# Filler matmuls, early moves and late checks around the first two attention units of a gated linear attention + multiplicative FFN kernel

## The chip, the cores and the metric

The kernel runs on one core of a Trainium2 chip, in one launch. The metric is the device time of that launch in microseconds (us), the median of 5 runs. Beside it there is one execution taken by the hardware profiler. Its engines are named as in the profile: PE (TensorE matmul), PEld (TensorE weight load), DVE (VectorE), ACT (ScalarE), POOL (GpSimd), SP (SyncE, which here issues every DMA).

## What is computed

```python
# attention: B, H, S, D = 4, 8, 768, 48
mag = sqrt(a_re**2 + a_im**2)
scale = minimum(mag, 0.999) / (mag + 1e-6)
a_re_n, a_im_n = a_re * scale, a_im * scale
for t in range(S):
    ar, ai = a_re_n[:, :, t, :, None], a_im_n[:, :, t, :, None]
    new_re, new_im = ar * S_re - ai * S_im, ar * S_im + ai * S_re
    S_re, S_im = new_re + k[:, :, t] (x) v[:, :, t], new_im
    y[:, :, t] = q[:, :, t] @ S_re
# FFN: x = y as (3072, 384); w1, w2 (384, 1024), w3 (1024, 1024), w_out (1024, 384)
out = ((x @ w1) * (x @ w2) @ w3) @ w_out
```

The four weights arrive as 64-bit floats, everything else as 32-bit floats.

## The kernel before, in words

The sequence of each of the 4 batches is cut in two, which gives 8 units (`NU`) of 384 time steps (`TT`); a unit is three chunks of 128 (`UC`). For every unit there are four kinds of work.

- **Gates** (`gates`, L531 to L643, a generator that is advanced one step at a time). ACT and DVE turn a_re and a_im into running products and angles and multiply q and k by them. Its lines that matter here: L554 (`im`, DVE, needs the loaded im), L559 (DVE), L544 (all its ACT activations), L567, L576 (scans), L600 (angle scans), L608, L616 to L620 (the last products). Its last step, "move" (L623 to L643), is 12 DMAs (L630) that rearrange k and q into KL and QL, heads beside each other, and then the loads of the next unit's k, q and v (`load_qkv`).
- **Attention** (`pieces`, L884): `turn` transposes k on PE into PSUM (tile tp, pool ps_v with 2 buffers) and ACT copies it to KT (L654); `state` multiplies KT by V (kv, L702) and DVE adds it to the running state T (L709); `scores` (sc, L664, pool ps_s with 2 buffers) needs KL and QL and is copied under the causal mask into one of two buffers A by DVE (L666); `outputs` (y, L691) needs A, T and QL, and ACT copies it to xT (L693). V is filled from the loaded vr by two ACT copies (L516).
- **FFN** (`ffn_ab`: the products with w1 and w2, tile m, L722, ACT copy a L727, DVE product ab L728, `KF` = 8 of them for a unit; `ffn_out`: tile o, L738, with w3o = w3 @ w_out, ACT copy L742 and store L744). Tiles m and o come from pool ps_m with 4 buffers.
- **Checks**: the kernel verifies that its inputs are in the range that its formulas allow. Two ACT activations per block of gates (`check_gates`, L518), and for units 0 and 1 and for all the weights a separate pass over freshly loaded data (`check_weights`, L786, tiles named look; ACT lines L520, L805, L806, L808). `judge` counts the verdicts at the end; a general slow path is behind a branch that isn't taken here.

Before the first FFN, w3o is made: 8 rows of w3 and w_out are loaded as raw 64-bit words (`row_work`, L829; tile raw, pool of 3 buffers, L758), converted by ACT (L764, L766, L770) and DVE (L768, L771, L773, L775) and multiplied on PE (`fuse`, L847, tile f). A row's w3 goes to a buffer of tag xT, of which there are two, so the conversion of row f+2 starts with a wait for PE's matmuls of row f. w1 and w2 are converted in four parts each in the same way, between the other work.

The order on PE is the order in which the Python code emits matmuls (`manual_schedule` for PE). On ACT, DVE and SP a scheduler orders the instructions ahead of time by priority and its own estimate of when they can start; on the chip each of these queues runs strictly in that fixed order, so an instruction that waits holds up all behind it. `high_priority` marks the copies out of PSUM.

The driver code is L914 to L985. After the first six rows of `fuse`, the last two rows are split: 8 matmuls for `j` 0 to 3, and four "fillers" of two matmuls each (`fill`, L941), which are put between the pieces of unit 0's attention after pieces 0, 1, 3 and 5. Then come unit 0's 8 `ffn_ab` (`rest[:HEAD]`), during which gates(1) takes its steps, and for each further unit `unit(u, ...)` (L900): `ahead` FFN parts of unit u-1 first (0 for unit 1, 3 for later ones), then the pieces of unit u with the rest of the previous unit's FFN spread evenly between them, one step of gates(u+1) after each part, and one `look` (for u > 1) after each piece.

Of the kernel before, what the change touches and what calls it, by code (L numbers as in the profile page):

```python
# [15 lines left out]
AF = mybir.ActivationFunctionType  # L16
OP = mybir.AluOpType
PSUM = bass.MemoryType.PSUM
ORDER = mybir.DependencyInfo(mybir.DependencyClass.NoSync, mybir.DependencyReason.DATA)
# [355 lines left out]
def kernel(  # L375
# [36 lines left out]
    nc = tc.nc  # L412
# [8 lines left out]
    KF = FF // P  # L421
# [21 lines left out]
    fast = ExitStack()  # L443
# [10 lines left out]
    gate_pool, head_pool = [one, None], [one, None]  # L454
# [11 lines left out]
    ONE, EPS, QUARTER, LEAST, MOST, TINY, TWO = (consts[:, i:i + 1] for i in range(7))  # L466
# [4 lines left out]
    st_low = singles.tile([P, 2, NU, KD], FP, name="st_low")  # L471
# [10 lines left out]
    def load_rows(dst, src, u, which=range(KD), queue=nc.sync):  # L482
        b, h = divmod(u, 2)
        for i, f in enumerate(which):
            queue.dma_start(out=dst[:, i, 0:TT], in_=src[b, :, DG * f:DG * (f + 1), h * TT:(h + 1) * TT].rearrange(  # L485
                "h d s -> d h s"))

    def load_gates(u):
        g = g_t.setdefault(u, {})
        for n, src in (("re", art), ("im", ait)):  # L490
            g[n] = one.tile([P, KD, TT], FP, tag=n, name=n)
            load_rows(g[n], src, u)
# [23 lines left out]
            nc.scalar.copy(out=V[:, :, :, i, e0:e0 + D], in_=vr[:, :, :, i])  # L516

    def check_gates(u, re, junk, f=0):  # L518
        for x, (scale, bias) in enumerate(((-1.0, LEAST), (1.0, MOST))):
            nc.scalar.activation(out=junk, in_=re, func=AF.Relu, scale=scale, bias=bias,  # L520
                                 accum_out=st_low[:, x, u, f:f + 1])

    chained = []

# [190 lines left out]
    def ffn_ab(u, j):  # L715
        if j == 0:
            ab_t[u] = one.tile([P, KF, TT], FP, tag="ab", name="ab")
        got = []
        for w in (w1s, w2s):
            m = ps_m.tile([P, TT], FP, tag="mm", name="m")  # L720
            for f in range(KD):
                nc.tensor.matmul(out=m, lhsT=w[:, j * P // WB, f, j * P % WB:j * P % WB + P], rhs=xT_t[u][:, f],  # L722
                                 start=(f == 0), stop=(f == KD - 1))
            got.append(m)
        a = two.tile([P, TT], FP, tag="a", name="a")
        with tc.high_priority():
            nc.scalar.copy(out=a, in_=got[0])  # L727
            nc.vector.tensor_tensor(out=ab_t[u][:, j], in0=got[1], in1=a, op=OP.mult)  # L728

    def ffn_out(u, t, parts=1):  # L730
# [46 lines left out]
    def load_weight(dst, src, halves=False):  # L777
        if src.dtype == FP:
            nc.sync.dma_start(out=dst, in_=src)
        else:  # L780
            convert(dst, src, halves)

    def words(src):
        return (src if src.dtype == FP else src.bitcast(I32)).rearrange("(i p) m -> p i m", p=P)

    def check_weights(late):  # L786

        for u in range(2):
            for f in range(KD):
                re = late.tile([P, 2, TT], FP, tag="look", name="look")  # L790
                load_rows(re, art, u, [f])
                check_gates(u, re[:, 0], re[:, 1], f)
                yield
        n = 0
        for w in (w1, w2, w3t, wo):
            if w.dtype == FP:
                continue
            src = words(w)
            step = min(src.shape[2], 1024)
            for i in range(src.shape[1]):  # L800
                for j in range(0, src.shape[2], step):
                    raw = late.tile([P, 512, 2], I32, tag="look", name="look")
                    nc.sync.dma_start(out=raw[:, 0:step // 2].rearrange("p m w -> p (m w)"), in_=src[:, i, j:j + step])
                    lo, hi = (raw[:, 0:step // 2, x].bitcast(FP) for x in range(2))
                    nc.scalar.activation(out=hi, in_=hi, func=AF.Square, scale=2.0 ** 15)  # L805
                    nc.scalar.activation(out=lo, in_=hi, func=AF.Relu, scale=-1.0, bias=TINY, accum_out=st_wts[:, n:n + 1])  # L806
                    if w is w3t:
                        nc.scalar.activation(out=hi, in_=hi, func=AF.Relu, bias=TWO, accum_out=st_wts[:, n + 40:n + 41])  # L808
                    n += 1
                    yield  # L810
# [3 lines left out]
    def rounding():  # L814

        stack = ExitStack()
        for n, k in (("raw", 3), ("low", 2)):
            cv[n] = stack.enter_context(tc.tile_pool(name=n, bufs=k))
        return stack

    def columns(src, j0, j1):
        n = 1 if src.dtype == FP else 2
        return words(src)[:, :, n * j0:n * j1]
# [5 lines left out]
    def row_work(f, parts=1):  # L829

        if f == 0:
            w3_t["wo"] = one.tile([P, KF, DM], FP, tag="ab", name="wo_s")
        w3_t[f] = two.tile([P, FF], FP, tag="xT", name="w3s")

        def some(n):
            step = FF // parts
            load_weight(w3_t[f][:, n * step:(n + 1) * step].rearrange("p (i m) -> p i m", i=1),
                        columns(w3t, n * step, (n + 1) * step)[:, f:f + 1], True)
        some(0)
        load_weight(w3_t["wo"][:, f:f + 1], words(wo)[:, f:f + 1])  # L840
        for n in range(1, parts):
            some(n)
# [34 lines left out]
        nc.vector.tensor_scalar(out=good, in0=count[:, 6:7], scalar1=float(P * need), scalar2=None, op0=OP.is_equal)  # L877

    for A in Ab:
        nc.gpsimd.memset(A, 0.0)  # L880
    for V in Vb:
        nc.gpsimd.memset(V, 0.0)

# [16 lines left out]
    def unit(u, steps, rest, look, ahead):  # L900

        for f in rest[:ahead]:
            f()
            next(steps, None)
        rest = rest[ahead:]
        p = pieces(u) + [[]]
        n = len(p)
        for i in range(n):
            for f in rest[i * len(rest) // n:(i + 1) * len(rest) // n] + p[i]:
                f()  # L910
                next(steps, None)
            next(look, None)

    gate_pool[1] = fast.enter_context(tc.tile_pool(name="late_gates", bufs=1))  # L914
    with tc.manual_schedule(engines={mybir.EngineType.PE}):

        phase = rounding()
        row_work(0, 2)
        load_gates(0)
        take_qk(0)  # L920
        steps = gates(0, True)
        for f in range(KF):
            if f:
                row_work(f)
            if f == 2:
                load_qkv(0)
            if f >= KF - 2:
                continue
            for j in range(KF):
                fuse(f, j)  # L930
            for _ in range(2):
                next(steps, None)
        work = w12_work()
        for f in work[:2]:
            f()
        for _ in steps:
            pass
        for f in range(KF - 2, KF):
            for j in range(KF // 2):
                fuse(f, j)  # L940
        fill = [lambda f=f, j=j: [fuse(f, j + x) for x in range(2)] for f in range(KF - 2, KF) for j in range(KF // 2, KF, 2)]  # L941
        load_gates(1)
        steps = gates(1, False)
        take_qk(1)
        rest = ffn(0, 2)
        work = work[2:]
        for i, p in enumerate(pieces(0)):
            for f in p:
                f()
            if i in (0, 1, 3, 5):  # L950
                fill.pop(0)()
            if i == 0:
                for f in work[:2]:
                    f()
                load_qkv(1)
            if i >= 2:
                next(steps)
            if i in (5, 7):
                work[2 + (i == 7)]()
        for i, f in enumerate(rest[:HEAD]):  # L960
            f()
            if i < 2:
                work[4 + i]()
            if i == 2:
                phase.close()
            if i < 6:
                next(steps)
        head_pool[1] = fast.enter_context(tc.tile_pool(name="late_heads", bufs=1))
        for _ in steps:
            pass  # L970
        load_gates(2)
        late = fast.enter_context(tc.tile_pool(name="late", bufs=2))
        look = check_weights(late)
        for u in range(1, NU):
            steps = gates(u + 1, False) if u + 1 < NU else iter(())
            unit(u, steps, rest[HEAD:] if u == 1 else ffn(u - 1), look if u > 1 else iter(()), AHEAD[u])
            for _ in steps:
                pass
            if u + 2 < NU:
                load_gates(u + 2)  # L980
        for _ in look:
            pass
        judge()
        for f in ffn(NU - 1):
            f()  # L985
# [41 lines left out]
```

## Time and profile before

| | |
|---|---|
| median of 5 runs | 589.92 us (588.52 to 594.95) |
| the profiled execution | 592.3 us, of which its span (first to last instruction) is 590.5 us |
| PE busy in the span | 553.0 us (94%), 3514 matmul records |
| DVE, ACT, POOL busy | 304.9, 349.6, 5.3 us |
| moved by DMA | 84.71 MB, mean 143 GB/s |
| mean granted PE clock | 0.994 |

The page of the profile cuts the span into 40 slices of 14.76 us and gives for each the busy share of every engine in tenths. A group line gives an engine's instructions of one kind, their summed busy time, the mean duration of one, and the idle time just before them with what ended it. A line of waits says which engine and line waited for which, the total, the number of times and the longest. A timeline line gives start, duration, engine, line, operation, output<-inputs, and in square brackets the idle time before it with its releaser. One program-level matmul in 32 bit shows as two records.

### The profile page before, as it was taken

Reading aid. Unit: us, or ns where it says so; the run is one execution under the profiler, and the core shown is the slowest. Engines: PE = TensorE matmul, PEld = TensorE weight load, DVE = VectorE, ACT = ScalarE, POOL = GpSimd, SP = SyncE. Lnnn points to the kernel's source line nnn. Section 1 sums busy time; section 2 is a strip of 40 time slices with the busy share of each in tenths; the row PEclk is TensorE's granted clock in tenths of the full one; section 3 lists DMA queues with packets and bytes.
Section 4 is the critical chain, followed back from the end, with each engine's and each line's share of the span. In section 5 each row is a group of like instructions: output and inputs, shape, how many; then the busy total and the mean of one; then the engine's idle time right before and its main releaser. Section 6 shows DMA issues by size and latency. Waiting matters only on the chain.

```text
span 590.5 us, 8844 instructions
## 1 busy us (share of the span) xinstructions
PE 553.0 (94%) x3514; PEld 364.9 (62%) x3514; DVE 304.9 (52%) x420; ACT 349.6 (59%) x572; POOL 5.3 (1%) x11
## 2 busy tenths in 40 slices
PE   4769989969899999999999999999999999999996
PEld 2435765548456765677567765776567656766553
DVE  6998488845761576158513674357415682310110
ACT  6897648566983699388834687498635742111100
POOL 3000000000000000000000000000000000000000
PEclk9889999999999999999999999999999999999999
DMA  8776998377385648652744348825820025000001
GB/s 296 265 295 217 247 294 279 108 183 214 122 235 117 186 136 244 127 180 87 191 114 112 117 135 188 245 78 160 199 73 1 14 68 120 1 15 29 0 1 44
DMA packets 46050, 84.71 MB, mean 143 GB/s; under 512 B 4656, under 2 KB 36144, under 8 KB 45104
## 3 DMA queue, kind: packets, MB, share of 16 engines
q1 hardware_dynamic: 46000, 84.06, 50.2%
q8 instruction: 29, 0.48, 0.3%
q14 instruction: 21, 0.17, 0.1%
HBM read 60.42 MB, written 4.72 MB: 110 GB/s over the span
## 4 chain that ended last, share of the span: by engine, by line
PE 62%; DVE 11%; DMA 10%; ACT 10%; issue 3%; SPq 3%; DVEq 0%; ACTq 0%
PE m L722 33%; PE o L738 16%; PE y L691 5%; PE sc L664 4%; DMA raw<-in_w_dram 4%; PE kv L702 3%; DMA QL<-gA 3%; ACT gZ L544 2%; PE tp L652 2%; SPq L485 2%; DVE gZ L600 2%; DMA vr<-in_v_dram 2%; ACT re L544 2%; DMA q<-in_q_dram 1%; DVE gA L576 1%
## 5 line engine op out<-in xcount | busy, mean ns | idle before, releaser
L722 PE MATMUL m<-xT,w1s 128*128 128x384 f32 x384 | 135.1, 488 | 3.9 <-ACT xT L693 3.9
L722 PE MATMUL m<-xT,w2s 128*128 128x384 f32 x384 | 134.5, 487 | 1.1 <-DVE w2s L775 0.6
L738 PE MATMUL o<-w3o,ab 128*128 128x384 f32 x384 | 130.1, 492 | 0.0
L728 DVE TENSOR_TENSOR ab<-m,a 128x384 f32<-128x384 f32 x64 | 35.5, 555 | 139.9 <-PE m L722 129.3
L722 PEld LDWEIGHTS m<-xT,w2s 128*128 128x128 f32 x384 | 72.8, 190 | 52.7 <-DVE w2s L775 1.2
L738 PEld LDWEIGHTS o<-w3o,ab 128*128 128x128 f32 x384 | 71.0, 190 | 48.5 <-issue 3.8
L722 PEld LDWEIGHTS m<-xT,w1s 128*128 128x128 f32 x384 | 70.3, 190 | 47.2 <-ACT xT L693 5.3
L727 ACT COPY a<-m 128x384 f32<-128x384 f32 x64 | 30.4, 475 | 75.7 <-PE m L722 75.6
L852 PE MATMUL f<-wo_s,w3s 128*128 128x384 f32 x128 | 48.9, 541 | 17.6 <-DVE wo_s L775 17.6
L654 ACT COPY KT<-tp 128x384 f32<-128x384 f32 x40 | 33.6, 845 | 43.5 <-PE tp L652 43.5
L664 PE MATMUL sc<-QL,KL 96*128 96x128 f32 x384 | 47.8, 278 | 2.8 <-DVE A L666 2.8
L664 PEld LDWEIGHTS sc<-QL,KL 96*128 96x128 f32 x384 | 45.6, 192 | 6.8 <-DVE A L666 4.1
L852 PEld LDWEIGHTS f<-wo_s,w3s 128*128 128x128 f32 x128 | 26.5, 213 | 37.3 <-DVE wo_s L775 19.7
L666 DVE COPY_PREDICATED A<-causal,sc 128x512 f32<-128x512 int32 x48 | 34.3, 734 | 15.4 <-PE sc L664 15.1
L691 PE MATMUL y<-A,V 128*32 128x128 f32 x768 | 39.2, 275 | 0.0
L691 PEld LDWEIGHTS y<-A,V 128*32 128x32 f32 x768 | 32.8, 109 | 5.7 <-issue 2.2
L691 PE MATMUL y<-QL,T 96*32 96x128 f32 x640 | 34.4, 272 | 0.0
L702 PEld LDWEIGHTS kv<-V,KT 128*96 128x96 f32 x320 | 29.6, 165 | 3.9 <-issue 2.7
L742 ACT COPY ot<-o 128x384 f32<-128x384 f32 x24 | 11.2, 466 | 35.2 <-PE o L738 35.2
L702 PE MATMUL kv<-V,KT 128*96 128x64 f32 x320 | 29.9, 246 | 1.4 <-ACT KT L654 1.4
L691 PEld LDWEIGHTS y<-QL,T 96*32 96x32 f32 x640 | 31.2, 110 | 0.0
L544 ACT ACTIVATE re<-gZ 128x1152 int32<-128x1152 f32 (+3 forms) x20 | 19.1, 967 | 15.2 <-DVE gZ L600 13.6
(98 smaller groups left out, 584.5 us busy)
## 6 DMA issues: line engine op xcount, KB each, us to landing
look<-in_w_dram SPq DMA_DIRECT2D x28, 512.0 KB, 4.9
raw<-in_w_dram SPq DMA_DIRECT2D x7, 1024.0 KB, 8.4
raw<-in_w_dram SPq DMA_DIRECT2D x8, 768.0 KB, 8.1
KL<-gR SPq DMA_DIRECT2D x24, 192.5 KB, 3.2
KL<-k SPq DMA_DIRECT2D x24, 192.5 KB, 3.7
re<-in_a_re_dram SPq DMA_DIRECT2D x24, 192.0 KB, 5.9
im<-in_a_im_dram SPq DMA_DIRECT2D x24, 192.0 KB, 3.5
k<-in_k_dram SPq DMA_DIRECT2D x24, 192.0 KB, 3.5
```

Of the source, the lines that this page charges most:

```text
L485: queue.dma_start(out=dst[:, i, 0:TT], in_=src[b, :, DG * f:DG * (f + 1), h * TT:(h + 1) * TT].rearrange("h d s -> d h s"))
L544: chain(nc.scalar.activation(**kw))
L654: nc.scalar.copy(out=KT_t[u, c][:, :, :, x].rearrange("p h d f -> p f d h"), in_=tp.rearrange("p f (d h) -> p f d h", h=H))
L664: nc.tensor.matmul(out=sc[:, j], lhsT=KL[:, x * n + j, w], rhs=QL[:, x * n + j, w], start=True, stop=True)
L666: nc.vector.copy_predicated(out=A[:, x * n:(x + 1) * n], data=sc, mask=causal.rearrange("p (h t) -> p h t", h=1).to_broadcast([P, n, C]))
L691: nc.tensor.matmul(out=o, lhsT=a, rhs=b, start=s0, stop=s1)
L702: nc.tensor.matmul(out=kv[:, hd], lhsT=KT[:, hd].rearrange("p d x f -> p (d x f)"), rhs=V[:, hd], start=True, stop=True)
L722: nc.tensor.matmul(out=m, lhsT=w[:, j * P // WB, f, j * P % WB:j * P % WB + P], rhs=xT_t[u][:, f], start=(f == 0), stop=(f == KD - 1))
L727: nc.scalar.copy(out=a, in_=got[0])
L728: nc.vector.tensor_tensor(out=ab_t[u][:, j], in0=got[1], in1=a, op=OP.mult)
L738: nc.tensor.matmul(out=m, lhsT=ab_t[u][:, f, t * P:(t + 1) * P], rhs=w3o[:, f], start=(f == 0), stop=(f == KF - 1))
L852: nc.tensor.matmul(out=sums[j], lhsT=w3_t[f][:, j * P:(j + 1) * P], rhs=w3_t["wo"][:, f], start=(f == 0), stop=(f == KF - 1))
```

## The change

- `row_work(0, 4)`: row 0 of w3 is loaded and converted in four parts instead of two.
- The two memsets of the A buffers (L880) go from POOL to DVE.
- The four fillers of unit 0 stand after pieces 1, 3, 6 and 9 instead of 0, 1, 3 and 5.
- In unit 1 the six halves of `ffn_out` are spread by a list, `first`, instead of evenly. Evenly they stood before pieces 1, 3, 4, 6, 8 and at the end; by the list they stand before pieces 0, 2, 4, 7 and two at the end.
- The pool of the late KL and QL buffers is made after the third `ffn_ab` of unit 0; the last step of gates(1) and `load_gates(2)` are emitted in the last turn of that loop instead of behind it.
- `follow`: the separate checks get an ordering dependency on the `ffn_ab` copy (L727) that was emitted last when the check is emitted, so the scheduler cannot put them ahead of it.

```diff
     def check_gates(u, re, junk, f=0):
-        for x, (scale, bias) in enumerate(((-1.0, LEAST), (1.0, MOST))):
-            nc.scalar.activation(out=junk, in_=re, func=AF.Relu, scale=scale, bias=bias,
-                                 accum_out=st_low[:, x, u, f:f + 1])
+        return [nc.scalar.activation(out=junk, in_=re, func=AF.Relu, scale=scale, bias=bias,
+                                     accum_out=st_low[:, x, u, f:f + 1])
+                for x, (scale, bias) in enumerate(((-1.0, LEAST), (1.0, MOST)))]
...
-            nc.scalar.copy(out=a, in_=got[0])
+            copied[:] = [nc.scalar.copy(out=a, in_=got[0])]
...
+    copied = []
+
+    def follow(work):
+
+        for ins in work:
+            tc.add_manual_dep(ins.ins, copied[-1].ins.name, ORDER, reason="later")
+
     def check_weights(late):
...
-                check_gates(u, re[:, 0], re[:, 1], f)
+                follow(check_gates(u, re[:, 0], re[:, 1], f))
...
-                    nc.scalar.activation(out=hi, in_=hi, func=AF.Square, scale=2.0 ** 15)
+                    follow([nc.scalar.activation(out=hi, in_=hi, func=AF.Square, scale=2.0 ** 15)])
...
     for A in Ab:
-        nc.gpsimd.memset(A, 0.0)
+        nc.vector.memset(A, 0.0)
...
         n = len(p)
+        first = [i * len(rest) // n for i in range(n + 1)] if u > 1 else [0, 1, 1, 2, 2, 3, 3, 3, 4, 4, 6]
         for i in range(n):
-            for f in rest[i * len(rest) // n:(i + 1) * len(rest) // n] + p[i]:
+            for f in rest[first[i]:first[i + 1]] + p[i]:
...
-        row_work(0, 2)
+        row_work(0, 4)
...
-            if i in (0, 1, 3, 5):
+            if i in (1, 3, 6, 9):
                 fill.pop(0)()
...
             if i == 2:
                 phase.close()
+                head_pool[1] = fast.enter_context(tc.tile_pool(name="late_heads", bufs=1))
             if i < 6:
                 next(steps)
-        head_pool[1] = fast.enter_context(tc.tile_pool(name="late_heads", bufs=1))
-        for _ in steps:
-            pass
-        load_gates(2)
+            if i == KF - 1:
+                for _ in steps:
+                    pass
+                load_gates(2)
```

## The prediction

> **What bounds the kernel now.** The page first: PE is busy 94% of the span.
>
> ```profile
> span 590.5 us, 8844 instructions
> PE 553.0 (94%) x3514; PEld 364.9 (62%) x3514; DVE 304.9 (52%) x420; ACT 349.6 (59%) x572; POOL 5.3 (1%) x11
> ...
> PE   4769989969899999999999999999999999999996
> ```
>
> The change takes no matmul away, so only PE's 37.5 idle us (590.5 - 553.0) can be won, and they lie in the slices below 9: the first twelve and the last. The waits of PE say on whom:
>
> ```profile
> PE f L852 <- DVE wo_s L775: 17.6, 4, 8.6
> PE tp L652 <- DVE gR L616: 4.9, 2, 3.5
> PE m L722 <- ACT xT L693: 3.9, 2, 2.5
> PE sc L664 <- DVE A L666: 2.8, 6, 1.2
> PE kv L702 <- ACT KT L654: 1.4, 1, 1.4
> ```
>
> PE's timeline gives the place of each:
>
> ```profile
> 37.08 20.02 PE L852 MATMUL f<-wo_s,w3s 128*128 128x384 f32 x56 [4.85 <-DVE wo_s L775]
> ...
> 78.69 2.05 PE L664 MATMUL sc<-QL,KL 96*128 96x128 f32 x16 [1.23 <-DVE A L666]
> ...
> 85.81 2.20 PE L722 MATMUL m<-xT,w1s 128*128 128x384 f32 x6 [1.41 <-ACT xT L693]
> ...
> 121.39 0.52 PE L652 MATMUL tp<-ident,gR 128*128 128x128 f32 x3 [3.51 <-DVE gR L616]
> ...
> 157.47 2.20 PE L722 MATMUL m<-xT,w1s 128*128 128x384 f32 x6 [2.52 <-ACT xT L693]
> ...
> 170.76 0.52 PE L652 MATMUL tp<-ident,gR 128*128 128x128 f32 x3 [1.41 <-DVE gR L616]
> ```
>
> Sums by stage: start 17.6 (8.60, 3.47, 4.85, 0.67); unit 0's attention 3.2; a wait of 0.57 for w2s at 111.8; unit 1's attention 7.9 (3.51, 1.38, 0.47, 2.52); unit 2's 1.41; all later units 1.4; the end 5.5, which the change doesn't touch. From 172 us on PE is full, so what arrives there earlier ends earlier. Last, ACT and DVE around the waits:
>
> ```profile
> 4.51 1.64 DVE L768 TENSOR_SCALAR w3s<-raw 128x512 int32<-128x512 int32 x1 [3.28 <-DMA raw<-in_w_dram]
> ...
> 76.65 1.36 DVE L554 TENSOR_TENSOR im<-im,gR 128x1152 f32<-128x1152 f32 x1 [1.67 <-DMA im<-in_a_im_dram]
> ```
>
> ```profile
> 88.72 1.25 ACT L516 COPY V<-vr 128x576 f32<-128x576 f32 x2 [2.96 <-DMA vr<-in_v_dram]
> ...
> 114.77 0.62 ACT L520 ACTIVATE look<-look,consts 128x384 f32<-128x384 f32 x1
> ...
> 118.61 1.24 ACT L544 ACTIVATE re<-re,consts 128x1152 f32<-128x1152 f32 x1
> ```
>
> **Start (row 0 in four parts, memsets to DVE).** The memsets of A: 951 ns each on POOL. On DVE, small memsets differ by 0.84 ns an element (128x80 125 ns, 128x24 78 ns), so about 0.9 each and 1.8 in all, in DVE's idle time from 1.17 to 4.51: hidden. If the first part lands earlier than 3.0, they cost the difference. POOL's two V memsets (1.38 each) then end near 4.2 instead of 5.87, and the first L768, 1.64 while they ran against 0.42 for its twin at 8.47, loses most of its 1.2 us. A first part of half the size lands up to 1 us earlier (512 KB took 3.8 us), and PE starts at 6.6 instead of 8.60. Splitting costs ACT 0.3 us (L764 0.78 for 512 columns, 1.35 for 1024, so some 0.1 for each extra piece of each kind), beside ACT's idle 1.86 at 8.18, and two more issues of 0.4 on SP, where the loads of re and im now stand behind parts that wait for a raw buffer. PE's early start isn't itself the gain: row 1 must come earlier too (ACT began it at 15.63, behind the gates), and the DMA engines were at or above 0.92 from 3 to 16 us, so row 1 can hardly be taken before 14.4: at most 1.2. Against that, DVE's new order puts row 5's L768 ahead of L635 and L639, and it waits for PE's row 3 (37.08 plus 6 records at the slow 0.64 and 10 at 0.32: 43.9, where DVE is there at 43.15). That passes some 0.7 on to row 7. I take -0.5; bounds -2.0 (PE's start passed on whole) and +1.5 (re and im late by two more landings of 0.75).
>
> At one place a rule can be weighed. PE's weight loads came every 0.64 us after the gap of 4.85 and every 0.32 from 40.7 on; after the gap of 3.51 at 121.39 the next eight o records took 2.75, full speed. The Trainium skill, "TensorE: Matmul & The Clock Gate", section "What's actually happening", has PE fall to half clock after an idle window of about 3.4 us and stay there for as long. By that rule the gap of 3.51 would bring 1.7 us more when it goes; by the row nothing, and the sum goes by the row.
>
> **Unit 0's fillers.** Four fillers of 1.3 us (4 records of 0.32). Removed: 0.23 before the second scores and 1.41 before the FFN. New: kv of chunk 2 has no filler ahead of it any more and waits for two KT copies (mean 0.85; the second starts when the transpose ends): 1.1. Scores reach PE earlier by two fillers less this wait, some 1.4 us; KL and QL landed close to 72 (last issue 64.96, 6.8 for its neighbour), but w1's raw load now goes out before six gate steps of DVE (6 x 0.47), so I let landings come 1 us earlier and add 0.4. More important are the new orders. DVE has L554 and L559 (1.27 each) both ahead of the A copies of chunk 1, where only L554 stood: the 1.23 stays. It has L771 of w2s, whose data landed at 82.9, ahead of the A copies of chunk 2: these end near 84.3, and y of chunk 2 waits about 1.0. And ACT has a V copy, which waited for vr until 88.7, ahead of the last xT copy: with vr at 87.7, V 0.57 and xT 0.48, m starts near 88.8, less the start's 0.5, so 88.3 against 85.81. I take +2.5 for all of it beyond the start's gain. Bounds: -1.6 (both old waits gone, nothing new) and +4.1 (vr lands as before: 88.7+0.57+0.48 = 89.8). The 0.57 for w2s goes: PE comes later and the conversions don't: -0.6 (bounds -0.6, 0).
>
> **Late checks and unit 1.** Here the gain lies. Between gates(1)'s L544 at 113.62 and 118.61 four L520 stand on ACT, 2.4 us. The changed order has none there, so L616 starts 2.4 earlier than 119.88 and ends near 118.7. PE arrives at 117.88-0.5+2.5-0.6 = 119.3 and does an o half first (8 records, 2.6 us): 3.51 goes to 0. The transposes of chunk 0 now have an o between them and kv: two KT copies, 1.5 us, fit into 2.6, and 1.38 goes. One o stands before the third scores: 0.47 goes. Two o halves (5.2) stand before m, where one didn't cover xT: 2.52 goes. New: nothing stands before y of chunk 2, and its A copies are behind L567 (1.27): 0.9. Sum 0.9-7.9 = -7.0. Bounds -7.9 and -3 (if gates(2) comes no earlier, all that PE gains before it is paid at y and at the transposes of unit 2).
>
> As to the moves: `HEAD` equals `KF`, so the last turn of the loop and the place behind it are one; in both orders the 12 moves of unit 1 precede the store. What pulls them is L616, and that two loads of look that waited for ACT no longer stand ahead of them on SP. Moves from 121.27 to about 118.5, and re of unit 2, issued at 130.13 and landed at 136.45, near 132. That starts gates(2) 4 us earlier, and its chain loses looks too (three, 1.8 us, from 142.73; one L806/L805 group later). L616 of unit 2 at 169.26 comes to about 163.5; PE, at 169.35 when it began to wait, comes to 169.35+1.4-7.0 = 163.8. So the 1.41 goes: -1.4 (bounds -1.4, 0).
>
> **Units 2 to 7.** The checks (all look lines, 81 us of ACT) stand later, between copies. ACT is 77% busy from 200 to 300 and PE idles 1.4 us in all after 172; m and o have four PSUM buffers. I take 0 (bounds -0.5, +2).
>
> **Sum.** -0.5+2.5-0.6-7.0-1.4 = -7.0. The profiled execution, 592.3 (span 590.5), would be 585.3. It lies 2.4 over the median of the runs, so the median goes from 589.92 to 582.9, and I say 583.
>
> **Rivals.**
> A: *the copies wait for transfers.* The landings aren't earlier, unit 0 pays 4.1 and gates(2) is pulled only by the removed looks, so that unit 1 gives -4.4 instead of -7.0: -0.5+4.1-0.6-4.4-1.4 = -2.8, so 587. For it: DVE and ACT sat idle on DMA at 76.65 and 88.72, and the new orders stand behind just those. Against it: w1's load goes out when DMA was at 0.65 (50 to 60 us).
> B: *the start carries through.* -2.0 at the start, unit 0 free (0), the rest as forecast: -2.0+0-0.6-7.0-1.4 = -11.0, so 579. Against it: ACT and DVE are 97 to 100% busy from 30 to 50 us.
> C, *on the other side:* the late checks hold up PE in units 2 to 7. There are 42 of them (6 + 36); each is some 1.4 us of ACT in one piece ahead of a KT, xT or a copy. If PE waits 0.17 us for each on average, the gain of 7.0 is gone; at 0.31 (13 us) it is 596. Against it: checks stand between copies now as well, and m waited for a just once, 0.53.
> That the edits do nothing: for the emission of the moves it is so, as said; the fillers' and checks' orders do differ.
>
> **Chances.** Forecast 50% (own range 580.5 to 585.5), A 26%, B 17%, C 7%. The range 578 to 588.5 leaves out C, the far end of A and of B, about 2 in 10. A measurement of this kernel tells about 1% from no change: 584.0 and 595.8. Faster than that: 30 of the forecast's 50 and B's 17, 47%. Within: 20, A's 26 and 2 of C, 48%. Slower: 5%.
>
> **What would show it.** Right: no gap above 1 us at the first transposes of unit 1 and 2; no L520 look on ACT before unit 2; m of unit 0 starting later than 85.8, behind a V copy; re of unit 2 landing near 132. Wrong: m of unit 0 before 85 (unit 0's loss isn't there), PE waiting for xT after unit 1, or gaps at L654 or L727 after 172.

## The result and the profile after

The changed kernel takes 589.96 us (median of 52 runs, 587.11 to 593.25); the kernel before, run beside it, 590.97 (94 runs). The ratio is 0.9984, 95% interval 0.9975 to 0.9992: faster, but by 1 us and not by 7, and outside the range 578 to 588.5. The profiled execution took 589.02 us, its span is 587.2; before it was 592.3 and 590.5. So the pair of profiles differs by 3.3 us and the medians by 1.0: the profile of before lies 1.3 above its median and that of after 0.9 below. The places below explain the 3.3; where the other 2.3 lie isn't shown, and what is said of time rests on the runs. One thing is known of that profile of before: its mean granted clock, 0.994, is above that of all 112 runs of before that were timed beside the experiments (0.978 to 0.991). It had less half clock than before usually has.

The page of the changed kernel first:

```profile
span 587.2 us, 8856 instructions
PE 554.7 (94%) x3514; PEld 366.9 (62%) x3514; DVE 306.4 (52%) x426; ACT 351.5 (60%) x576; POOL 3.5 (1%) x9
...
PE   4579899999979999999999999999999999999996
PEclk9789999999989999999999999999999999999999
```

PE idles 32.5 us (587.2 - 554.7) instead of 37.5, and some of its busy time is longer: in the twelfth slice (162 to 176 us) PE shows a 7 and PEclk an 8. PE's waits name the places:

```profile
PE f L859 <- DVE wo_s L775: 19.6, 4, 7.3
PE tp L652 <- DVE gR L616: 3.2, 1, 3.2
PE sc L664 <- DVE A L666: 1.3, 4, 0.4
PE m L722 <- ACT xT L693: 1.2, 1, 1.2
PE kv L702 <- ACT KT L654: 0.9, 1, 0.9
```

The start has grown from 17.6 to 19.6; the waits for A, xT and KT have shrunk from 8.1 in all to 3.4; 3.2 for L616 stay, but at another unit, as PE's timeline shows:

```profile
22.43 12.66 PE L859 MATMUL f<-wo_s,w3s 128*128 128x384 f32 x32 [6.87 <-DVE wo_s L775]
...
60.46 1.88 PE L859 MATMUL f<-wo_s,w3s 128*128 128x384 f32 x5 [1.32 <-DVE wo_s L775]
...
88.16 2.20 PE L722 MATMUL m<-xT,w1s 128*128 128x384 f32 x6 [1.18 <-ACT xT L693]
...
166.53 0.83 PE L652 MATMUL tp<-ident,gR 128*128 128x128 f32 x3 [3.24 <-DVE gR L616]
167.16 3.52 PE L722 MATMUL m<-xT,w1s 128*128 128x384 f32 x6
```

Row 1 of w3 is ready at 22.43 (before 19.95), row 7 at 60.46 (57.77). Between 88 and 166 us no gap is over 0.8: unit 1's four gaps are filled. Then PE stands for 3.24 us at unit 2's transposes, where it stood for 1.41, and the six m records behind that gap take 3.52 instead of the 2.10 or 2.20 that six take elsewhere: they run at half clock. The windows of that stretch say the same (their column before the last two is the granted clock):

```profile
164.00:166.00 2.00, 0.00 (x0) 0.00 (x0) 1.40 (x2) 2.00 (x2) 0.00 (x0) 1.00 0.00 0
166.00:168.00 2.00, 1.47 (x5) 1.19 (x6) 2.00 (x3) 1.97 (x4) 0.00 (x0) 0.65 0.14 31
168.00:170.00 2.00, 2.00 (x5) 1.08 (x4) 2.00 (x3) 1.88 (x5) 0.00 (x0) 0.50 0.99 261
170.00:172.00 2.00, 2.00 (x7) 1.19 (x7) 0.66 (x1) 1.26 (x4) 0.00 (x0) 1.00 0.94 231
```

Step by step, by PE's position in the two profiles:

| PE reaches | before | after | this step | forecast |
|---|---|---|---|---|
| row 7 of `fuse` | 57.77 | 60.46 | +2.69 | -0.5 |
| unit 0's first m | 85.81 | 88.16 | -0.34 | +2.5 |
| the end of unit 0's `ffn_ab` (w2s) | 117.88 | 119.39 | -0.84 | -0.6 |
| the first m behind unit 1's attention | 157.47 | 151.52 | -7.46 | -7.0 |
| unit 2's first transposes | 170.76 | 166.53 | +1.72 | -1.4 |
| the end of the span | 590.5 | 587.2 | +0.93 | 0 |

The sum is -3.3 against -7.0. The first two rows belong together (+2.35 for +2.0, below), unit 1 is near the forecast; what is missing is lost at unit 2 and at half clock behind it: 1.72 + 1.4 + 0.93 = 4.05, of which the first four rows give back 0.35.

Unit 2's transposes wait for the product L616, and its chain starts with the load of re. Before, and then after:

```profile
130.13 1.88 SPq L485 DMA_DIRECT2D re<-in_a_re_dram  x3
136.50 1.17 ACT L544 ACTIVATE gA<-re 128x1152 f32<-128x1152 f32 x1 [4.50 <-DMA re<-in_a_re_dram]
169.26 1.36 DVE L616 TENSOR_TENSOR gR<-k,re 128x1152 f32<-128x1152 f32 x1 [1.79 <-ACT re L544]
```

```profile
126.87 1.88 SPq L485 DMA_DIRECT2D re<-in_a_re_dram  x3
165.03 1.36 DVE L616 TENSOR_TENSOR gR<-k,re 128x1152 f32<-128x1152 f32 x1 [0.60 <-ACT re L544]
```

(The line of ACT of after, at 134.05, stands further below, beside that of e14.)

### The profile page after: what moved, and what is told of

It reads as the page before. It is cut to its first block, busy times and chain, and to the rows that moved or that the text cites. A ratio compares the mean times of both kernels' runs of the same rounds, so it can differ in the third digit from the quotient of the medians.

```text
span 587.2 us, 8856 instructions
## 1 busy us (share of the span) xinstructions
PE 554.7 (94%) x3514; PEld 366.9 (62%) x3514; DVE 306.4 (52%) x426; ACT 351.5 (60%) x576; POOL 3.5 (1%) x9
## 4 chain that ended last, share of the span: by engine, by line
PE 73%; DVE 10%; DMA 8%; ACT 4%; issue 3%; SPq 1%; ACTq 0%; DVEq 0%
PE m L722 36%; PE o L738 19%; PE y L691 5%; DMA raw<-in_w_dram 5%; PE sc L664 5%; PE kv L702 4%; PE tp L652 2%; PE f L859 2%; DMA vr<-in_v_dram 2%; ACT re L544 1%; DVE gZ L600 1%; DMA re<-in_a_re_dram 1%; DVE gA L576 1%; DMA k<-in_k_dram 1%; DVE k L589 1%
## 5 line engine op out<-in xcount | busy, mean ns | idle before, releaser
L727 ACT COPY a<-m 128x384 f32<-128x384 f32 x64 | 30.5, 477 | 70.7 <-PE m L722 70.6
L859 PE MATMUL f<-wo_s,w3s 128*128 128x384 f32 x128 | 49.7, 548 | 19.6 <-DVE wo_s L775 19.6
L691 PEld LDWEIGHTS y<-QL,T 96*32 96x32 f32 x640 | 31.3, 110 | 0.0
L544 ACT ACTIVATE re<-gZ 128x1152 int32<-128x1152 f32 (+3 forms) x20 | 19.1, 967 | 18.2 <-DVE gZ L600 14.4
```

The source lines that it names most:

```text
L544: chain(nc.scalar.activation(**kw))
L691: nc.tensor.matmul(out=o, lhsT=a, rhs=b, start=s0, stop=s1)
L727: copied[:] = [nc.scalar.copy(out=a, in_=got[0])]
L859: nc.tensor.matmul(out=sums[j], lhsT=w3_t[f][:, j * P:(j + 1) * P], rhs=w3_t["wo"][:, f], start=(f == 0), stop=(f == KF - 1))
```

## The experiments

All kernels were timed against the kernel before on the same chip. "Row 1, row 7" are the times at which PE could start on these rows; "L616" is the start of that product for unit 1 and for unit 2; "gap" is PE's wait at unit 2's first transposes.

| kernel | median, us | before | ratio, interval | row 1, row 7 | L616: unit 1, 2 | gap |
|---|---|---|---|---|---|---|
| before | - | - | 1 | 19.95, 57.77 | 119.9, 169.3 | 1.41 |
| after | 589.96 | 590.97 | 0.9984 (0.9975-0.9992) | 22.43, 60.46 | 117.6, 165.0 | 3.24 |
| e1 two parts | 589.51 | 590.33 | 0.9978 (0.9958-0.9999) | 20.28, 58.80 | 116.8, 164.1 | 3.23 |
| e2 memsets on POOL | 590.71 | 590.33 | 0.9989 (0.9967-1.0011) | 23.20, 62.55 | 119.8, 167.2 | 3.23 |
| e10 one raw buffer | 588.61 | 590.93 | 0.9958 (0.9939-0.9978) | 19.75, 59.58 | 116.8, 164.4 | 3.25 |
| e3 late checks alone | 587.72 | 590.33 | 0.9950 (0.9924-0.9977) | 20.48, 59.25 | 117.1, 164.1 | 0 |
| e13 the same again | 587.68 | 590.93 | 0.9935 (0.9908-0.9963) | 20.22, 58.86 | 117.1, 164.0 | 0 |
| e4 unit 1's list alone | 593.89 | 590.86 | 1.0059 (1.0037-1.0080) | 19.88, 57.26 | 119.8, 168.8 | 3.39 |
| e11 late checks, list | 589.03 | 590.93 | 0.9964 (0.9945-0.9984) | 19.73, 58.34 | 117.3, 164.8 | 3.23 |
| e12 late checks, unit 0's fillers | 588.21 | 590.93 | 0.9955 (0.9932-0.9979) | 20.33, 58.33 | 117.8, 164.8 | 0 |
| e17 late checks, one raw buffer | 588.00 | 590.90 | 0.9948 (0.9928-0.9969) | 20.90, 58.45 | 117.8, 164.8 | 0 |
| e8 dummy matmuls | 588.84 | 590.33 | 0.9960 (0.9939-0.9981) | 21.92, 62.54 | 119.5, 167.0 | 0 |
| e6 four parts ahead | 589.67 | 590.86 | 0.9987 (0.9968-1.0006) | 22.30, 61.34 | 118.4, 165.9 | 0 |
| e7 the same, two parts | 589.72 | 590.86 | 0.9982 (0.9963-1.0000) | 19.60, 59.27 | 118.4, 165.8 | 0 |
| e9 late checks, list, four ahead | 589.37 | 590.86 | 0.9975 (0.9951-0.9999) | 19.13, 58.72 | 117.3, 164.7 | 0 |
| e14 re first | 621.69 | 590.90 | 1.0527 (1.0495-1.0559) | 22.70, 62.24 | 119.1, 160.6 | 0 |
| e15 re first, one raw buffer | 615.94 | 590.90 | 1.0421 (1.0392-1.0450) | 20.23, 59.90 | 116.0, 155.2 | 0 |
| e16 late checks, re first | 616.56 | 590.90 | 1.0438 (1.0410-1.0466) | 20.14, 58.50 | 116.6, 157.0 | 0 |

My theory after the result: the four parts of row 0 delay the start, the chain of gates(2) sets when unit 2 may begin, whatever PE saves before, and the new gap brings half clock. The rival is that unit 1's fillers, or the late checks, are a loss by themselves.

### The parts of the change

**e1**, after with row 0 in two parts again:

```diff
-        row_work(0, 4)
+        row_work(0, 2)
```

> The changed kernel with row 0 of w3 in two parts again. In the profile of the change PE got row 1 at 22.43 us instead of 19.95 and row 7 at 60.46 instead of 57.77. Theory 1 (four parts hold up SP: re and im stand behind parts that wait for a raw buffer): row 1 comes back to 20 or earlier, row 7 to about 57.8, and the time falls by 2 to 2.7 against the change, to about 587.5 (ratio to before 0.994). Rival (the memsets on DVE, or the new order of DVE around row 5, make the start late): row 1 stays near 22, the time near 590 (0.998).

Row 3 of w3 starts 2.15 us earlier than in after (36.97 for 39.12) and row 7 1.66 (58.80 for 60.46); between them PE was at half clock for longer, 0.50 from 36 to 42 us, and the 56 records from row 3 on took 21.16 where before and after both have 20.02. L616 of unit 2 comes only 0.9 earlier and the gap is 3.23 again, so the 2 to 2.7 us that I expected did not come. The ratio is 0.0006 below after's, well inside the intervals: what the start gives back goes into waits further on.

**e2**, after with the memsets of A on POOL:

```diff
     for A in Ab:
-        nc.vector.memset(A, 0.0)
+        nc.gpsimd.memset(A, 0.0)
```

> The changed kernel with the memsets of A on POOL again, four parts kept. Theory 1: the start stays late, row 1 at 22 to 23 us, the first L768 is slow again if POOL still runs beside it, time within 1 us of the change (590, ratio 0.998). Rival (memsets on DVE make the start late): row 1 at 20, time 587.5 (0.994).

Rows 1 and 7 come no earlier than in after. The memsets' move is not what delays the start.

**e3** and **e13**, before with the late checks alone (`check_gates` returns its instructions, `copied`, `follow`, and its two uses, as in the diff of the change):

```diff
-                check_gates(u, re[:, 0], re[:, 1], f)
+                follow(check_gates(u, re[:, 0], re[:, 1], f))
...
-                    nc.scalar.activation(out=hi, in_=hi, func=AF.Square, scale=2.0 ** 15)
+                    follow([nc.scalar.activation(out=hi, in_=hi, func=AF.Square, scale=2.0 ** 15)])
```

> Before, with the late checks alone. Theory 2 (the checks held up the gates of units 1 and 2): L616 of unit 1 ends 2.4 us earlier and the wait of 3.5 at the first transposes of unit 1 falls to about 1; the wait after unit 1 for xT shrinks; time 2.5 to 4 below before (587 to 588.5, ratio 0.994 to 0.996). Rival (fillers alone do it, PE is bound elsewhere): within 0.7 us of before (ratio 0.999 to 1.001).

> Late checks alone once more, beside the others, so that the two kernels that add one edit to it are compared with it on the same chip. My theory: ratio to before 0.993 to 0.997 again. Rival (the first time was a lucky one): 0.997 to 1.000, as the whole change.

Both times this one edit gives more than the whole change: 2.6 and 3.3 us below before. PE's timeline of the first:

```profile
118.65 0.52 PE L652 MATMUL tp<-ident,gR 128*128 128x128 f32 x3 [2.52 <-DVE gR L616]
...
153.99 2.20 PE L722 MATMUL m<-xT,w1s 128*128 128x384 f32 x6 [2.00 <-ACT xT L693]
...
165.70 0.49 PE L652 MATMUL tp<-ident,gR 128*128 128x128 f32 x3
```

Unit 1 keeps its gaps (2.52, 0.71, 0.83, 2.00), and just therefore PE comes to unit 2's transposes at 165.70, when L616, started at 164.14, has just ended (165.50): no wait, no half clock.

**e4**, before with the list of unit 1 alone:

```diff
+        first = [i * len(rest) // n for i in range(n + 1)] if u > 1 else [0, 1, 1, 2, 2, 3, 3, 3, 4, 4, 6]
         for i in range(n):
-            for f in rest[i * len(rest) // n:(i + 1) * len(rest) // n] + p[i]:
+            for f in rest[first[i]:first[i + 1]] + p[i]:
```

> Kernel before with the list of filler positions in unit 1 alone. My theory (the idle time filled in unit 1 comes back as a wait of unit 2's transposes for the product L616, because the chain of gates(2) sets that time, and the late checks are what shortens that chain): L616 of gates(2) stays near 169 us as before, PE is at unit 2's transposes some 5 us earlier than before's 170.76, so they wait 3 to 6 us, a stretch at half clock may follow, and the time is within 1.5 us of before (589 to 592, ratio 0.998 to 1.003). Rival (filling unit 1 is a gain by itself and the checks do nothing): 584.5 to 587, ratio 0.990 to 0.995.

It is slower than I expected, 3.0 us above before. L616 of unit 2 stays at 168.8:

```profile
121.32 0.52 PE L652 MATMUL tp<-ident,gR 128*128 128x128 f32 x3 [1.04 <-DVE gR L616]
124.28 0.87 PE L652 MATMUL tp<-ident,k 128*128 128x128 f32 x3 [2.44 <-issue]
170.26 0.52 PE L652 MATMUL tp<-ident,gR 128*128 128x128 f32 x3 [3.39 <-DVE gR L616]
```

Unit 2 begins at 170.26 for 170.76, so the filled gaps are nearly all back in one, and there are two stretches at half clock (0.66 from 120 to 130 us, 0.66 from 170 to 175) that the profile of before didn't have. In the six timed runs of e4 the mean granted clock was 0.981, in the 29 of before beside them 0.986. The list is a loss without the late checks.

**e11** and **e12**, the late checks with one edit more: e11 the list of e4, e12

```diff
-            if i in (0, 1, 3, 5):
+            if i in (1, 3, 6, 9):
```

> Kernel before with the late checks and the list of filler positions in unit 1, and nothing else. Late checks alone gave 0.995 and no wait at unit 2's transposes. My theory: the list takes 3 to 4 us of waits out of unit 1, but L616 of gates(2) stays near 164 us, so PE waits there for 2.5 to 4 us, with a stretch at half clock behind it in most profiles; the time is 1 to 2.5 us above late checks alone (589 to 590.5, ratio 0.997 to 1.000). Rival (the list is worth something beside the late checks): 585 to 587, ratio 0.990 to 0.994.

> Kernel before with the late checks and the four fillers of unit 0 after pieces 1, 3, 6 and 9. My theory: small; the waits of unit 0's attention (about 3 us before) fall by 0.5 to 1.5 us, half of which unit 2's wait for L616 takes back; within 1 us of late checks alone (586.7 to 588.7, ratio 0.993 to 0.997). Rival (the later fillers leave an early gap bare, as I predicted for the whole change): 589 to 591, ratio 0.997 to 1.001.

Beside e13 on the same chip, both medians are higher, by 1.35 and 0.5 us; the intervals overlap, so a small loss is likely but not settled. What is settled is the place: e11 waits 3.23 us at unit 2 (and still 1.96 and 1.29 in unit 1); e12 has no wait there, keeps unit 1's 0.71, 0.83 and 1.99, and needs 29.99 us from row 7 to unit 0's first m, where e13 needs 25.65 (58.86 to 84.51). PE and ACT of e12 show why:

```profile
80.00 2.05 PE L664 MATMUL sc<-QL,KL 96*128 96x128 f32 x16 [1.52 <-DVE A L666]
...
88.32 2.20 PE L722 MATMUL m<-xT,w1s 128*128 128x384 f32 x6 [1.13 <-ACT xT L693]
```

```profile
87.22 0.67 ACT L516 COPY V<-vr 128x576 f32<-128x576 f32 x1 [2.73 <-DMA vr<-in_v_dram]
87.80 0.47 ACT L693 COPY xT<-y 128x384 f32<-128x384 f32 x1
```

The last xT copy stands behind a V copy that waits for vr, and m comes 1.1 us after vr. PE then reaches unit 1 at 119.39 without a wait; e13, there at 116.0, waits 2.56 for L616 until 118.56. So of 3.8 us at m 0.8 are left at unit 1.

The early emission of the moves was not run by itself. That it changes no order is argued in the prediction and not shown by a run.

### Why the start is late

SP's own timeline of after shows it (issue time, duration):

```profile
2.12 0.70 SPq L485 DMA_DIRECT2D re<-in_a_re_dram  x1
5.30 0.34 SPq L758 DMA_DIRECT2D raw<-in_w_dram  x1
5.69 0.58 SPq L485 DMA_DIRECT2D re<-in_a_re_dram  x1
6.66 0.33 SPq L758 DMA_DIRECT2D raw<-in_w_dram  x1
7.04 0.55 SPq L485 DMA_DIRECT2D re<-in_a_re_dram  x1
7.63 1.88 SPq L485 DMA_DIRECT2D im<-in_a_im_dram  x3
9.62 0.52 SPq L758 DMA_DIRECT2D raw<-in_w_dram  x1
```

Three raw buffers are taken by parts 0 and 1 and by w_out's row, so part 2 waits until 5.30 and part 3 until 6.66, and two of re's three loads, im and row 1 stand behind them: row 1 is issued at 9.62, in before at 6.23. From 6 to 10 us the DMA engines' busy share is 0.73, in before 1.08. **e10** gives row 0's parts four slices of one raw buffer:

```diff
         w3_t[f] = two.tile([P, FF], FP, tag="xT", name="w3s")
+        whole = cv["raw"].tile([P, 1, FF, 2], I32, tag="raw", name="raw") if parts > 1 else None
...
-                        columns(w3t, n * step, (n + 1) * step)[:, f:f + 1], True)
+                        columns(w3t, n * step, (n + 1) * step)[:, f:f + 1], True,
+                        whole[:, :, n * step:(n + 1) * step] if parts > 1 else None)
```

> Kernel after, but the four parts of row 0 are loaded into four slices of one raw buffer, so that no part waits for a raw buffer and the loads of re, im and row 1 aren't queued behind it on SP. My theory (the start is late because SP's queue stands behind parts that wait for a buffer): row 1 is ready at 19.5 to 20.5 us (after 22.4, before 19.95) and row 7 at 57.5 to 59 (after 60.5); the time is 0 to 1.5 us below after (588.5 to 590), because the wait of unit 2's transposes for L616 takes most of it. Rival (four smaller transfers are slower whatever the queue does): row 1 stays at 22 or later, row 7 at 60 or later.

```profile
1.64 1.38 SPq L759 DMA_DIRECT2D raw<-in_w_dram  x3
3.06 1.96 SPq L485 DMA_DIRECT2D re<-in_a_re_dram  x3
5.07 1.89 SPq L485 DMA_DIRECT2D im<-in_a_im_dram  x3
7.00 0.59 SPq L759 DMA_DIRECT2D raw<-in_w_dram  x1
```

Nothing waits now: row 1 is issued at 7.00 and ready at 19.75. Over all kernels the split is clean: with four parts in buffers of their own row 1 came at 21.9 to 23.2 (after, e2, e6, e8, e14), otherwise at 19.1 to 20.9. Row 7, at 59.58, missed the 57.5 to 59 that I expected; the 56 records ahead of it took 21.02 us. e10's median is 1.35 below after's, the spans of the profiles differ by 0.5 only (586.7 and 587.2), and the two intervals overlap a little: a gain is likely, not settled. PE's earlier first matmul (7.38) doesn't carry: row 1 is no earlier than with two parts. **e17** puts e10's edit on e13, with two parts:

> Kernel before with late checks, and row 0's two parts loaded into two halves of one raw buffer, so that the load of row 1 waits for no buffer. My theory: row 1 is ready 0 to 1 us earlier than 20.2 to 20.5, row 7 0 to 1.5 us earlier than 58.9 to 59.3, time 0 to 1 us below late checks alone: ratio 0.992 to 0.996. Rival (the transfers are what is late, not their issue): no change at row 1 and the same ratio as late checks alone.

Row 1 at 20.90, the ratio as with late checks alone: with two parts the third buffer was no limit.

### Is the gap at unit 2 worth anything, and what sets it?

**e8**, after with four matmuls that nobody reads, ahead of unit 2's attention, so that PE works in the gap:

```diff
+        if u == 2:
+            m = ps_m.tile([P, TT], FP, tag="mm", name="warm")
+            for i in range(4):
+                nc.tensor.matmul(out=m, lhsT=ident, rhs=w3o[:, i], start=True, stop=True)
         p = pieces(u) + [[]]
```

> The changed kernel with four more matmuls (8 records of 128x384 on ident and w3o into a PSUM tile that nothing reads) ahead of unit 2's first transposes, where PE waits 3.24 us for L616 and then runs at half speed for 3.4 us. Theory 3 (the clock gate): the wait shrinks to 0.6 but the transposes start at the same time, and the records after them come every 0.32 us at once; the time falls by 1.7 against the change, to 588.3 (ratio 0.9955). Rival (the slow records after the wait are not the wait's doing, or the gate's window runs free and hits elsewhere): no change, or up to 0.7 slower (ratio 0.998 to 1.000).

```profile
165.84 2.85 PE L916 MATMUL warm<-w3o,ident 128*128 128x384 f32 x8 [0.58 <-ACT a L727]
168.52 0.49 PE L652 MATMUL tp<-ident,gR 128*128 128x128 f32 x3
168.85 2.10 PE L722 MATMUL m<-xT,w1s 128*128 128x384 f32 x6
```

L616 is no earlier for it, only PE is warm: the six records behind take 2.10 for 3.52, and the median stands 1.1 us under after's (the ratios, 0.9960 and 0.9984, have intervals that overlap a little). In the profile of after the tp and m records behind the gap took 0.31 and 1.42 longer, 1.7 in all.

**e6, e7, e9** cover the gap with one FFN part more ahead of unit 2: e6 is after with that, e7 has two parts in row 0 besides, e9 is before with late checks, the list and that.

```diff
-    AHEAD = [0, 0] + [3] * (NU - 2)
+    AHEAD = [0, 0, 4] + [3] * (NU - 3)
```

> Kernel after with four FFN parts of unit 1 ahead of unit 2's attention instead of three, so that 4.2 us more of matmuls cover the wait of unit 2's transposes (3.24 us, and about 1.7 us of half clock behind it). My theory: that wait and the half clock go, and the time falls by 3 to 5 us against after, to 585 to 587 (ratio to before 0.991 to 0.995). Rival (what the time lost lies elsewhere, at the start, or what is taken ahead is missing as a filler between unit 2's pieces): a new wait of 2 to 4 us inside unit 2 and the time within 1 us of after, 589 to 591.

> As the kernel with four parts ahead, but with row 0 in two parts as in before. My theory: with the wait for gates(2) covered, the start's 1.7 us (row 1 at 20.3 instead of 22.4, row 7 at 58.8 instead of 60.5) now reaches the end: 1 to 2 us below the kernel with four parts ahead, 584 to 586, ratio 0.989 to 0.993. Rival (the start's delay is swallowed at unit 0's attention whatever comes behind it): within 0.5 us of the kernel with four parts ahead.

> Kernel before with three edits only: late checks, the list of filler positions in unit 1, and four FFN parts ahead of unit 2. Late checks alone gave 0.995. My theory: filling unit 1 is worth 3 to 5 us once the wait for gates(2) is covered, so 583.5 to 586, ratio 0.988 to 0.992, with no wait over 1 us between 120 and 170 us. Rival (the late checks gave all that there was, and the fillers only move a wait): 587 to 588.5, ratio 0.994 to 0.997.

The rivals of these expectations hold: no better than after (e6, e7), and e9 is above the late checks alone (and kept waits of 1.96 and 1.33 us in unit 1, where I expected none over 1). The gap is gone, but further on, where after has none, e6's timeline has two new ones (e7 and e9 have the same two, 2.12 and 1.69, 1.23 and 1.68):

```profile
224.95 2.20 PE L722 MATMUL m<-xT,w2s 128*128 128x384 f32 x6 [1.62 <-ACT a L727]
...
358.74 0.52 PE L652 MATMUL tp<-ident,gR 128*128 128x128 f32 x3 [1.70 <-DVE gR L616]
```

The second is once more a wait for L616, at a later unit. In e9 PE reaches unit 2's transposes at 167.50 with one FFN part (3.9 us) more done than e3 has at 165.70, so 2.1 us ahead; the waits that follow in e9 and not in e3 (0.59, 1.23 and 1.68) are 3.5 in all, and its span is 1.6 us longer (586.4 and 584.8). What PE is spared at one unit, it meets at later copies and at the next gates.

The table says why. From L616 of unit 1 to L616 of unit 2 it is 49.4 us in before and 48.9 in e4; with late checks 47.0 to 47.6 in every kernel above e14 in the table, whatever the fillers are. **e14** goes for that distance: after, with the loads of re of unit 2 emitted before unit 1's moves (they come out behind the first of them).

```diff
         yield "move"

+        if u == 1:
+            load_gates(2)
         KL = head_pool[u % 2].tile([2 * D, H, TT + 1], FP, tag="KL", name="KL")
...
                 for _ in steps:
                     pass
-                load_gates(2)
```

> Kernel after, with the loads of re of unit 2 issued after the first of unit 1's moves instead of after the last. In after re was issued at 126.87, ACT took it at 134.05 after 5.97 us of idle time, and L616 of gates(2) started 31.0 us later, at 165.03. My theory (the landing of re sets the whole chain of gates(2)): ACT takes re 4 to 7 us earlier, L616 starts at 158.5 to 162, and the wait of 3.24 us at unit 2's transposes falls below 0.5; unit 1's scores wait up to 2 us longer for KL and QL; time 1 to 4 us below after (586 to 589). Rival (the chain is bound by ACT and DVE, shared with unit 1's copies): L616 comes less than 2 us earlier, the wait stays over 1.5, time within 1 us of after.

ACT of after, and then of e14:

```profile
134.05 1.17 ACT L544 ACTIVATE gA<-re 128x1152 f32<-128x1152 f32 x1 [5.97 <-DMA re<-in_a_re_dram]
```

```profile
128.15 1.17 ACT L544 ACTIVATE gA<-re 128x1152 f32<-128x1152 f32 x1 [2.79 <-DMA re<-in_a_re_dram]
```

re is taken 5.9 us earlier and L616 of unit 2 starts at 160.57, 32.4 later (31.0 in after): L616 moves with re, and the distance falls to 41.5. DVE's order changed too, as shown next, but that did not shorten the way from re to L616: it is 32.8 us in before, 30.6 in e3, and in e15 and e16 31.3 and 32.6. So the landing of re sets the chain. The time, however, rises by 5%, which neither theory had. PE and DVE of e14:

```profile
138.12 2.02 PE L666 MATMUL sc<-QL,KL 96*128 96x128 f32 x16 [0.85 <-DMA out_dram<-ot]
166.42 3.78 PE L666 MATMUL sc<-QL,KL 96*128 96x128 f32 x16 [26.28 <-DVE A L668]
```

```profile
137.31 0.69 DVE L711 TENSOR_TENSOR T<-kv,T 96x512 f32<-96x512 f32 x1 [1.66 <-PE kv L704]
137.92 1.34 DVE L567 SCALAR_TENSOR_TENSOR gA<-gZ,gA 128x1152 f32<-128x1152 f32 x1
...
164.38 1.35 DVE L620 TENSOR_TENSOR q<-q,gZ 128x1152 f32<-128x1152 f32 x1
165.65 1.32 DVE L668 COPY_PREDICATED A<-causal,sc 128x512 f32<-128x512 int32 x2
```

In the order that was fixed ahead of time DVE does all of gates(2), L567 to L620, before the first copy A of unit 1's scores. PE has its first scores at 138, and the next can't start until A is copied out of PSUM: 26.28 us. **e15** (e14 with e10's edit) and **e16** (e13 with e14's edit) have the same gap, 25.41 and 21.02:

> Both mends of after together: the four parts of row 0 in one raw buffer, and re of unit 2 loaded after the first move. My theory: the start's 1.5 to 2.5 us, which the wait for gates(2) took, now reach the end: 1 to 2.5 us below the kernel with re first, 585 to 587.5, ratio to before 0.990 to 0.994. Rival (the gain at the start is lost at unit 0 or 1 whatever comes behind): within 0.5 us of the kernel with re first.

> Kernel before with late checks, and re of unit 2 loaded after the first move of unit 1. Late checks alone had no wait at unit 2's transposes, so by my theory an earlier gates(2) has nothing to give: ratio 0.993 to 0.997 as late checks alone, perhaps 1 us worse by later KL and QL. Rival (the earlier re shortens later chains too): 0.989 to 0.992.

So these three show what sets L616, and not what an earlier re is worth; that stays open, as it would need the A copies kept ahead of the gates on DVE, which wasn't tried. Whether the start's loss reaches the end once the gap is gone isn't settled by them either; e7 beside e6 says mostly no: row 7 is 2.07 earlier, unit 0's first m, tied to vr, only 0.17 (88.80 and 88.97).

## Why the prediction was wrong

- **Start, -0.5: wrong, +2.69 at row 7**, and beyond the bound of +1.5. The text saw re and im behind parts that wait for a raw buffer and priced this as two landings of 0.75 at worst; row 1 itself, which stands behind them too, was issued 3.4 us later (9.62 for 6.23), and row 3 started 2.04 later (39.12 for 37.08). The other 0.65 is a longer wait at row 7 (1.32 for 0.67), near the 0.7 forecast for L768's wait for row 3. The memsets were as forecast (0.91 each, in DVE's idle time). e10 shows the cause at row 1, e2 excludes the memsets.
- **Unit 0, +2.5: right by position, with some luck.** The text had m at 88.3, because the last xT copy stands behind a V copy that waits for vr; V started at 87.06, xT ended 1.1 later, and m started at 88.16. That the step shows as -0.34 is the start's doing: m is tied to vr, so PE's late arrival is swallowed there. Both steps together are +2.35, forecast +2.0, so the start's error cost 0.35. The luck is in the sum: the text took 0.5 off for an early start that didn't come, and vr landed 0.6 before its 87.7.
- **Unit 1, -7.0: right, -7.5.** All four gaps went (one of 0.79, at the first scores, is new), and no look stands on ACT before L616.
- **Unit 2, -1.4: wrong, +1.72, and this decided it.** The step was "L616 of unit 2 at 169.26 comes to about 163.5; PE [...] comes to 163.8". It carried 3.1 of the 3.7 us between forecast and profile. Two things failed in it. 163.5 is the start of L616; its 1.36 us were left out, so by the prediction's own numbers PE had to wait 1.1. And re landed 2.45 us earlier, not 4: it was issued 3.3 earlier (126.87 for 130.13) and then took 0.8 longer, likely because the DMA engines were busier from 120 to 130 us, 1.05 for 0.78. So L616 came at 165.03, while PE, with unit 1's gain, was there at 163.29. The removed looks were as forecast: 31.0 from ACT's take of re to L616, before 32.8.
- **The clock: one row was too few.** The text priced a gap of 3.51 without half clock. It forecast no gap at unit 2, so this price didn't make the sum wrong by itself; but once the gap of 3.24 stood, half clock added 1.7 us, which less before's later wait of 0.53 for a, which went, is 1.2, near the +0.93 in the last row. The row came from the one profile of before, whose clock, 0.994, none of those 112 runs reached. The rule that the text weighed and set aside, the Trainium skill's "TensorE: Matmul & The Clock Gate", section "What's actually happening", also says that the window is free-running and that the number of slow matmuls varies from run to run. e3 and e13 agree: they are one kernel, and after waits of 2.00 and 1.99 us at the same place e3 ran at full clock and e13 at 0.50 from 156 to 158 us.
- **Rivals.** A was the nearest in time (587), and in part in cause: gates(2) came less early than forecast, though re did land earlier, and unit 1 gave all that was forecast. C didn't come: from 200 to 450 us after has two gaps of 0.30, and e3 and e13, with all checks late, have the lowest medians.
- **What should have been asked.** Unit 1's gain can only last as far as gates(2) come earlier. L616 of unit 2 moved by 4.2 us (169.26 to 165.03); that is the most that could have reached the later units, half clock took 1.7 of it, and 2.5 to 3.3 is what the pair of profiles shows. The bound of unit 1 in the prediction (-3, "paid at y and at the transposes of unit 2") was near this case; it was taken for the end and not for the rule.

The version to keep is the late checks alone: 587.7 us, 0.9950 and 0.9935 of before, below the whole change (0.9984) both times; the first interval just touches that of the whole change, the second lies clear of it.

## To carry to other kernels

A filled gap is a gain only if what the next stage waits for comes earlier too: measure the distance between two products of the chain that feeds PE (here 47 us from L616 to L616), and take no more than it shortens. Compare the end of the producer with the consumer's arrival, not its start. Splitting a load into more parts than the pool has buffers puts every later load of that queue behind the conversion (here row 1, issued at 9.62 for 6.23).

## What the hardware showed that was not expected

Half clock after a wait is not a matter of the wait's length alone. After waits of 3.23 to 3.25 us at the same place the m records were at half clock in after, e1, e2 and e10 (six in 3.3 to 3.8 us) and at full clock in e11 (2.10); after 3.51 us in before at full clock. And after 1.99 or 2.00 us at the first m behind unit 1 they ran at full clock in e3 and e12, at half in e13 and e17:

```profile
153.87 3.11 PE L722 MATMUL m<-xT,w1s 128*128 128x384 f32 x6 [1.99 <-ACT xT L693]
156.77 2.93 PE L722 MATMUL m<-xT,w2s 128*128 128x384 f32 x6
```

(e13; e3 took 2.20 and 2.10 there with the same order of instructions.) The page named above has half clock begin after at least one idle window of about 3.4 us; here 1.99 us were enough in two profiles of four, so idle time alone doesn't tell it. The runs of after fit a part that varies by execution: at a mean granted clock of 0.991 they took 587.1 to 588.3 us, at 0.977 592.2 to 593.0.
